# Differences of kept weights written to the exponentials' tile, at other steps, and two result rows leaving one group later

## The chip, the cores and the metric

One core of a Trainium2 chip runs the whole program. The metric is the device time of one execution in microseconds, the median of the runs shown. TensorE (PE) multiplies matrices, VectorE (DVE) and ScalarE (ACT) work element by element, GpSimd (POOL) and SyncE (SP) here only issue transfers.

## What is computed

```python
def _attn_ref(q, k, v, phi) -> np.ndarray:
...
    k_m = np.einsum('bhsm,bhsd->bhmd', a, k)
    v_m = np.einsum('bhsm,bhsd->bhmd', a, v)
...
    scores = scale * np.matmul(q, k_m.transpose(0, 1, 3, 2))
...
    return np.matmul(attn, v_m).astype(np.float32)
...
def _moe_ref(x, w_gate, w_val, w_out) -> np.ndarray:
    gate = 1.0 / (1.0 + np.exp(-(x @ w_gate)))
    val = x @ w_val
    return (gate * val @ w_out).astype(np.float32)
```

`a` is the softmax of `phi` over 32 memory slots, `attn` that of the scores. There are 8 batches of 8 heads, 576 positions, 64 wide; the attention's output is turned into 4608 tokens of 512 and goes through the gated layer of width 1536. The weights come in as 64-bit words and are turned into 32-bit floats on the chip.

## The kernel before, in words

The hidden width of 1536 is cut into 12 slices of 128. A **unit** is one batch and one slice: a gate (`gate_half`, two halves of columns), sigmoid on ACT, product on DVE (`product`, L711), rounding to a high part on ACT (`g_hi`, L721) and the rest on DVE (`g_lo`, by `rest`, L184), and later the product with the output weights into four accumulators (`out_half`). Batches 0 to 2 go through the slices in three turns of four (units 0 to 35 of `steps`); what has been summed after a turn leaves as a row (`leave`, from L766 on) to a buffer in memory and comes back as `row<-part` to be added on DVE (L771). Batches 3 to 7 then take all slices in one turn, in groups of another arithmetic (`Group`), with sums and differences of operands.

Those late batches need the gate weights once more, with the lower head of each pair as a difference of two halves. So in six of the units 0 to 35, listed in `KEEP_W`, two slices of weights are **kept**: SP issues two copies from the weights' tile (`wgv<-wg`, 512 KB and 256 KB), DVE makes two differences of 64 x 512 (L1247), and SP issues them as two transfers of 128 KB (`wgv<-row` before).

What sets the order: the first 12 units and the late batches are written out by hand. Between them, a scheduler places each engine's instructions by its own estimate of when they are ready. Each engine runs its list strictly in order, so an instruction that waits holds everything behind it. `move` (L173 to L180) issues nearly all loads and stores of this stretch on SP's queue, in program order.

Tiles come from pools with a fixed number of buffers; a new tile waits until every reader of the old one in its buffer is done. `row` has four, shared by rows that leave, rows that return, and (before) the differences. `e`, which holds the exponentials of a softmax, has one. The gates use four PSUM banks, `pu_t`: a unit's first half takes one, its second half two, so the second half of a unit takes a bank that the previous unit's first product has read. `acc0` to `acc3` are the four accumulators, one bank each, free when their row has been added (L771).

In the late loop (from L1409 on), `leave_late` adds and stores what is in `leaving`, twice per group: in the middle (L1458) and near the end (L1508).

Of the kernel before, what the change touches and what calls it, by code (L numbers as in the profile page):

```python
# [9 lines left out]
F32 = mybir.dt.float32  # L10
# [7 lines left out]
P = 128  # L18
B, H, S, D, M = 8, 8, 576, 64, 32
DM, DFF = 512, 1536  # L20
NG = 2
NKT = 4
# [18 lines left out]
QUAD = 3  # L41
# [62 lines left out]
def attn_moe_kernel(  # L104
# [15 lines left out]
    mb = ctx.enter_context(tc.tile_pool(name="moe", bufs=1))  # L120
# [19 lines left out]
    def att(shape, name, bufs=1):  # L140
        return sb.tile(shape, F32, name=name, bufs=bufs)
# [32 lines left out]
    def move(dst, src, queue="batch"):  # L174


        with ExitStack() as behind:
            if queue in last_move:
                behind.enter_context(tc.issue_after(last_move[queue].ins))
            last_move[queue] = queues[queue].dma_start(dst, src)  # L180
# [141 lines left out]
    def convert(f, k):  # L322
        to_f32(whole_of(f, k), f, k)
        if k == 2:
            wo_hi(f)
            wo_lo(f)
# [34 lines left out]
    def load_q(b, cuts=(0, 1)):  # L361
        if (b, "q") not in loaded:
            loaded[b, "q"] = att([P, NKT * S], "q")
        for c in cuts:
            for u, n in PIECES[c]:
                o = u * NKT * 2 * P
                move(loaded[b, "q"][:, o : o + NKT * n], qT[b][:, o : o + NKT * n])
# [235 lines left out]
    def again(b):  # L603
        new_at(b)
        for d, a in zip(kept[b], at[b]):
            move(a.rearrange("p r n -> p (r n)").bitcast(F32), d)
# [131 lines left out]
    def gate_all(b, f, c):  # L738
        for do in (gate_half, sigmoid, product, g_hi, g_left, g_lo):
            do(b, f, c)  # L740
# [52 lines left out]
    def row_of(b, t):  # L793

        st = mb.tile([P, DM], F32, name="row", bufs=4)
        if (b, t) in part:
            move(st, part[b, t])
        return st
# [6 lines left out]
    def out_left(pair, f0, nf):  # L805

        if pair:
            hi, lo = [mb.tile([P, TURN, P], F32R, name=f"left_{p}", tag="row", bufs=4) for p in ("hi", "lo")]
        else:
            hi, lo = [t.rearrange("p r f x -> p (r f x)").rearrange("p (f x) -> p f x", x=P) for t in u_tiles()]  # L810
        for k in range(0, nf, TURN):
            raw = left.pop((pair, (f0 + k) // TURN))
            nc.scalar.copy(hi[:, k : k + TURN], raw)
            if pair:
                yield
            rest(lo[:, k : k + TURN], raw, hi[:, k : k + TURN])
        yield
        ends_it = f0 + nf == NFT
        n = DM // 2 if ends_it and pair == B // 2 - 1 else DM
        if f0 == 0:  # L820
            left_sum[pair] = mb.tile([P, DM], F32, name="wo_raw")
        for x in range(0, DM, n):
            xs = slice(x, x + n)
            st, o = left_sum[pair][:, xs], (late_bank("c") if x else bank())[:, :n]
            for k in range(nf):
                w_hi, w_lo = [w[:, xs] for w in wo_of(f0 + k)]
                matmul(o, hi[:, k], w_hi, start=(k == 0), stop=False)
                matmul(o, hi[:, k], w_lo, start=False, stop=False)
                matmul(o, lo[:, k], w_hi, start=False, stop=(k == nf - 1))
            if "banks" in pools and n == DM:  # L830
                yield
            if f0 == 0:
                nc.vector.tensor_copy(st, o)
                continue
            nc.vector.tensor_tensor(st, o, st, op=ALU.add)
            if not ends_it:
                continue
            for j in range(2):
                b = 2 * pair + j
                to = out[b * S + SF * P : (b + 1) * S, xs]  # L840
                move(to, st[j * TAIL : (j + 1) * TAIL, :], ("batch", "act")[j] if pair == B // 2 - 1 else "batch" if pair else "stream")
        yield


    def run(*parts):
        for p in parts:
            for _ in p:
                pass
# [7 lines left out]
    @contextmanager  # L856
    def queued():

        traced = nc.cur_bb.bb.instructions
        at = traced[-1]  # L860
        with ExitStack() as behind:
            for ins in tail_of.values():
                behind.enter_context(tc.issue_after(ins))
            yield
        start = next(k for k in reversed(range(len(traced))) if traced[k] is at) + 1
        for ins in traced[start:]:
            if ins.engine in ORDERED:
                tail_of[ins.engine] = ins

    def step(do, *args, **kw):  # L870
        with queued():
            return do(*args, **kw)
# [162 lines left out]
            yield  # L1035

    MAIN = begin[QUAD, 0]
    KEEP_W = {17: 0, 18: 1, 19: 2, 20: 3, 25: 5, 28: 4}
    sides = {
        begin[0, TURN]: [(6, remember(QUAD, True))],  # L1040
        begin[1, NFT - TURN]: [(3, pause(3)), (3, score(QUAD, QUAD + 1))],
# [39 lines left out]
    def load_pair(n):  # L1081

        if n >= NPAIRS:
            return
        in_ring[n] = lp[0].tile([P, 2, NKT, 256], F32, name="ring")
        move(in_ring[n].rearrange("p f k n -> p (f k n)"), kept_w[n % NP])
# [142 lines left out]
    for i, (b, f, at_start, at_end) in enumerate(steps[:MAIN]):  # L1229
        if i < LISTED:  # L1230
            continue
        if i in sides:
            run(beside)
            beside, pieces = chain(*(g for _, g in sides[i])), sum(n for n, _ in sides[i])
            length = next(n for n in range(i + 1, len(steps) + 1) if n == len(steps) or steps[n][2]) - i
            slots = 2 * length - 1 - sum(i <= n < i + length for n in quad_at)
        if i in returns:
            again(returns[i])
        if i in KEEP_W:
            k = KEEP_W[i]  # L1240
            w, kept_k = wg[:, 2 * k : 2 * k + 2], kept_w[k].rearrange("p (f k n) -> p f k n", f=2, k=NKT)
            move(kept_k[D:], w[D:])
            move(kept_k[:D, :, :, :P], w[:D, :, :, :P])
            for j in range(2):
                t = mb.tile([P, DM], F32, name="row", bufs=4)[:D]
                t = t.rearrange("p (k n) -> p k n", k=NKT)
                nc.vector.tensor_tensor(t, w[:D, j, :, :P], w[:D, j, :, P:], op=ALU.subtract)  # L1247
                move(kept_k[:D, j, :, P:], t)
        if i == begin[1, NFT - TURN] - 1:
            load_q(QUAD)  # L1250
        if i == MAIN - 2:
            for t in range(SF):
                rows[b, t] = row_of(b, t)
        if i == MAIN - TURN:
            weights.close()
            lp[0] = weights.enter_context(tc.tile_pool(name="late2", bufs=1, side="right", reuse_waits="tile"))
            load_pair(0)
        extra = out_left(*lefts[i]) if i in lefts else iter(())
        gate_all(b, f, 0)
        due = list(CONVERT.get(i, ()))  # L1260
        while due and i not in quad_at:
            with behind():
                convert(*due.pop(0))
        next(extra, None)
        if i in u_at:
            if steps[i + 1][0] != b:
                run(beside)
            make_u(*u_at[i])
            part_u(*u_at[i])
        while len(pend) >= LAG:  # L1270
            out_half(*pend.pop(0))
        pend.append((b, f, 0, at_start, at_end))
        go_on()
        gate_all(b, f, 1)
        while due and due[0][1] != 2:
            with behind():
                convert(*due.pop(0))
        if i == MAIN - 3:
            with behind():
                first_hi(QUAD, 0)  # L1280
                first_lo(QUAD, 0)
                sums_at(QUAD, 1, 2, 3, 4)
        while len(pend) >= LAG and i < MAIN - 1:
            out_half(*pend.pop(0))
        if i in quad_at:
            quad(i)
            while due:
                with behind():
                    convert(*due.pop(0))
        if i == MAIN - 2:  # L1290
            pair_u(0, [bank(), bank()])
            for name in "rl":
                u_out(0, name)
            u_sums(0, 0, 1, 2)
            for name in "lrs":
                part_hi(0, name)
                part_lo(0, name)
        pend.append((b, f, 1, at_start, at_end))
        next(extra, None)
        if i not in quad_at:  # L1300
            go_on()
        del U[b, f]
# [109 lines left out]
    for b, f in [(b, f) for b in range(QUAD, B) for f in range(NFT)]:  # L1412
# [7 lines left out]
        n = (b - QUAD) * NP + f // 2  # L1420
# [84 lines left out]
        to_lo_done = h and b == QUAD and len(leaving) > 0  # L1505
        if to_lo_done:
            step(h.to_lo)
        step(leave_late)  # L1508
        if late_left:
            step(next, extra, None)  # L1510
        last = b == B - 1 and f == NFT - 1
# [97 lines left out]
```

## Time and profile before

| what | us |
|---|---|
| median of 3 runs (717.38 to 717.57) | 717.55 |
| the profiled execution | 718.11 |
| its span in the trace | 716.3 |
| PE busy in the span | 705.1 |
| DVE busy | 554.7 |
| ACT busy | 445.6 |
| all 16 transfer engines, mean | 172 GB/s |

The span is what the trace covers; some 1.8 us of the profiled execution's time lie around it. PE is busy 98% of the span at the full granted clock in every slice, so time can only be gained or lost where PE stands idle, or by giving it other work.

### The profile page before, as it was taken

The page shows a single profiled execution, that of the slowest core. Times are in us where ns is not written, and L with a number is a line of the kernel's source. Part 1 is how long each engine was busy: PE and PEld are TensorE (multiplying, and loading weights), DVE is VectorE, ACT ScalarE, POOL GpSimd, SP SyncE. Part 2 cuts the span into 40 slices and gives each one's busy share as a digit, 9 for nine tenths or more (in the row PEclk, how much of TensorE's full clock was granted, in tenths as well). Part 3 has the DMA queues.
Part 4 walks back from the last instruction along what each step waited for, and adds up shares of the span by engine and source line. Part 5 has one row for each costly group of instructions (what it writes and reads, how often), then busy time and mean ns, then how long its engine had stood idle before and what let it go on. Part 6 is the DMA issues. An engine that isn't in the chain of part 4 may idle for free.

```text
span 716.3 us, 14525 instructions
## 1 busy us (share of the span) xinstructions
PE 705.1 (98%) x5645; PEld 581.4 (81%) x5645; DVE 554.7 (77%) x1108; ACT 445.6 (62%) x1037; POOL 27.6 (4%) x55
## 2 busy tenths in 40 slices
PE   8999999999999999999999999999999999999997
PEld 7655898888988888878878888888888888788786
DVE  5898998778787676587888868787797778987663
ACT  4655776543354354466877567765777657686553
POOL 0000100111101110100000000000000000000000
PEclk9999999999999999999999999999999999999999
DMA  8966559878956835733166112752223422151102
GB/s 347 405 259 210 213 193 378 289 267 272 319 182 196 275 117 184 262 104 112 60 231 236 60 60 89 254 184 67 93 93 116 154 92 75 60 176 60 60 1 73
DMA packets 36084, 123.22 MB, mean 172 GB/s; under 512 B 3952, under 2 KB 11376, under 8 KB 28848
## 3 DMA queue, kind: packets, MB, share of 16 engines
q1 hardware_dynamic: 31296, 106.71, 42.2%
q0 software_dynamic: 4560, 15.47, 6.2%
q8 instruction: 44, 0.72, 0.4%
q14 instruction: 24, 0.20, 0.1%
q10 hardware_dynamic: 160, 0.13, 0.1%
HBM read 96.73 MB, written 25.56 MB: 171 GB/s over the span
## 4 chain that ended last, share of the span: by engine, by line
PE 86%; DMA 6%; DVE 4%; ACT 2%; SPq 1%; issue 1%; POOL 0%; DVEq 0%
PE acc L194 36%; PE pu_t L194 17%; PE c L194 11%; PE a L194 8%; PE b L194 7%; PE d L194 7%; DMA kvm<-in_kvm_dram 2%; DMA words<-in_wo_dram 1%; DMA row<-part 1%; DMA out_dram<-row 1%; SPq L180 1%; DMA part<-row 1%; DVE row L771 1%; DVE u_lo L184 1%; DVE row L1247 0%
## 5 line engine op out<-in xcount | busy, mean ns | idle before, releaser
L194 PE MATMUL acc<-wo_hi,g_hi 128*128 128x512 f32 x372 | 151.4, 407 | 0.0
L194 PE MATMUL acc<-wo_hi,g_lo 128*128 128x512 f32 x372 | 147.1, 395 | 0.0
L194 PE MATMUL acc<-wo_lo,g_hi 128*128 128x512 f32 x372 | 146.7, 394 | 0.0
L194 PE MATMUL pu_t<-at,u_hi 128*128 128x320 f32 (+1 forms) x560 | 116.7, 305 | 1.1 <-DVE e L512 1.1
L194 PEld LDWEIGHTS pu_t<-at,u_hi 128*128 128x128 f32 x560 | 92.1, 188 | 9.8 <-issue 2.1
L194 PEld LDWEIGHTS acc<-wo_hi,g_hi 128*128 128x128 f32 x372 | 69.8, 188 | 29.4 <-issue 9.7
L194 PEld LDWEIGHTS acc<-wo_hi,g_lo 128*128 128x128 f32 x372 | 69.9, 188 | 17.4 <-DVE g_lo L184 0.3
L194 PE MATMUL pu_t<-at,u_lo 128*128 128x256 f32 (+1 forms) x264 | 77.6, 294 | 0.0
L194 PEld LDWEIGHTS acc<-wo_lo,g_hi 128*128 128x128 f32 x372 | 70.1, 188 | 5.4
L1197 ACT COPY c_p<-c 128x288 f32<-128x288 f32 x60 | 23.9, 398 | 63.1 <-PE c L194 62.4
L169 ACT ACTIVATE sg<-pu_t 128x256 f32<-128x256 f32 (+1 forms) x70 | 28.5, 410 | 50.8 <-PE pu_t L194 46.5
L1201 DVE TENSOR_TENSOR z<-a,c_s 128x288 f32<-128x288 f32 x60 | 27.1, 452 | 32.9 <-PE a L194 32.8
L194 PEld LDWEIGHTS pu_t<-at,u_lo 128*128 128x128 f32 x264 | 49.6, 188 | 0.0
L721 ACT CAST g_hi<-sg 128x256 fp32r<-128x256 f32 x66 | 26.5, 405 | 36.5 <-DVE sg L711 34.6
L711 DVE TENSOR_TENSOR sg<-pu_t,sg 128x320 f32<-128x320 f32 (+1 forms) x69 | 31.1, 454 | 23.3 <-ACT sg L169 13.8
L169 ACT ACTIVATE z<-z 128x288 f32<-128x288 f32 x120 | 47.9, 441 | 1.5 <-DVE z L1201 0.8
L1201 DVE TENSOR_TENSOR z<-c,c_x 128x288 f32<-128x288 f32 x60 | 27.3, 455 | 27.3 <-PE c L194 24.5
L1213 ACT CAST g_hi<-z 128x512 fp32r<-128x512 f32 x60 | 37.4, 623 | 17.0 <-DVE z L1208 16.8
L184 DVE TENSOR_TENSOR g_lo<-z,g_hi 128x512 fp32r<-128x512 f32 x60 | 41.0, 684 | 2.5 <-ACT g_hi L1213 2.5
L194 PE MATMUL c<-ring,vT 64*32 64x512 f32 x232 | 31.4, 601 | 0.0
L194 PE MATMUL a<-ring,vT 64*32 64x512 f32 x232 | 31.4, 601 | 0.0
L1208 DVE TENSOR_TENSOR z<-z 128x288 f32<-128x288 f32 x60 | 27.0, 450 | 5.4 <-ACT z L169 0.8
(243 smaller groups left out, 1636.8 us busy)
## 6 DMA issues: line engine op xcount, KB each, us to landing
ring<-wgv SPq DMA_DIRECT2D x30, 1024.0 KB, 4.9
kvm<-in_kvm_dram SPq DMA_DIRECT2D x14, 1024.0 KB, 8.8
at<-at SPq DMA_DIRECT2D x18, 576.0 KB, 8.1
q<-in_qT_dram SPq DMA_DIRECT2D x16, 512.0 KB, 4.9
part<-row POOLq DMA_DIRECT2D x24, 256.0 KB, 5.0
row<-part SPq DMA_DIRECT2D x24, 256.0 KB, 3.8
words<-in_wo_dram SPq DMA_DIRECT2D x8, 512.0 KB, 9.6
words<-in_wgv_dram SPq DMA_DIRECT2D x4, 1024.0 KB, 5.1
```

Of the source, the lines that this page charges most:

```text
L169: last_act[0] = nc.scalar.activation(*args, **kw)
L180: last_move[queue] = queues[queue].dma_start(dst, src)
L184: return nc.vector.tensor_tensor(lo, x, hi.bitcast(F32), op=ALU.subtract)
L194: last_pe[0] = do(*args, **kw)
L711: last_prod[0] = nc.vector.tensor_tensor(prod, ps[1][:, :n], sg[:, :n], op=ALU.mult)
L721: nc.scalar.copy(hi, prod[:, : 2 * P])
L771: nc.vector.tensor_tensor(st, o, st, op=ALU.add)
L1197: copy(getattr(self, name), self.c if name == "p5" else self.d)
L1201: nc.vector.tensor_tensor(self.z[:, i], x, y, op=ALU.add)
L1208: nc.vector.tensor_tensor(self.z[:, 2 + i], x, self.z[:, i], op=ALU.mult)
L1213: nc.scalar.copy(self.g[0], self.z[:, 2:4, : 2 * P])
```

## The change

`KEEP_W` gives the unit at which a pair of slices is kept. Pair 4 moves from unit 28 to unit 22; the other five stay. The two differences of a pair now lie side by side in one tile of the name `e`, with one buffer, in place of two of the four `row` buffers. And in group 1 of batch 3, the late call of `leave_late` is left out, so the two rows that wait there leave at the call in the middle of group 2.

```diff
-    KEEP_W = {17: 0, 18: 1, 19: 2, 20: 3, 25: 5, 28: 4}
+    KEEP_W = {17: 0, 18: 1, 19: 2, 20: 3, 22: 4, 25: 5}
...
             move(kept_k[D:], w[D:])
             move(kept_k[:D, :, :, :P], w[:D, :, :, :P])
+            diff = att([P, 2 * S], "e")[:D, : 2 * DM].rearrange("p (f k n) -> p f k n", f=2, k=NKT)
             for j in range(2):
-                t = mb.tile([P, DM], F32, name="row", bufs=4)[:D]
-                t = t.rearrange("p (k n) -> p k n", k=NKT)
+                t = diff[:, j]
                 nc.vector.tensor_tensor(t, w[:D, j, :, :P], w[:D, j, :, P:], op=ALU.subtract)
                 move(kept_k[:D, j, :, P:], t)
...
-        step(leave_late)
+        if (b, f) != (QUAD, 1):
+            step(leave_late)
```

The instructions of PE keep their order, row for row. DVE's list moves at three places. The first is on DVE around the begin of unit 16: `u_lo` x4 are the rests of the operands of units 16 to 19, the next `sg` of 256 is unit 16's first product, the four rows from `acc_1682` on are the sums of batch 0 that leave. Before:

```order
L184 TENSOR_TENSOR u_lo<-pu_t,u_hi 128x512 x4
L711 TENSOR_TENSOR sg<-pu_t,sg 128x256
L273 TENSOR_SCALAR wg<-wg 128x512
L276 TENSOR_SCALAR wg<-wg 128x512
L184 TENSOR_TENSOR g_lo<-sg,g_hi 128x256
L711 TENSOR_TENSOR sg<-pu_t,sg 128x320
L280 SCALAR_TENSOR_TENSOR wg<-words_90,wg 128x512
L771 TENSOR_TENSOR row<-acc_1682,row 128x512
L771 TENSOR_TENSOR row<-acc_1686,row 128x512
```

And now, from the same `u_lo` on:

```order
L184 TENSOR_TENSOR u_lo<-pu_t,u_hi 128x512 x4
L1247 TENSOR_TENSOR e<-wg 64x512 x2
L711 TENSOR_TENSOR sg<-pu_t,sg 128x256
L273 TENSOR_SCALAR wg<-wg 128x512
L711 TENSOR_TENSOR sg<-pu_t,sg 128x320
L276 TENSOR_SCALAR wg<-wg 128x512
L771 TENSOR_TENSOR row<-acc_1682,row 128x512
L184 TENSOR_TENSOR g_lo<-sg,g_hi 128x256
L771 TENSOR_TENSOR row<-acc_1686,row 128x512
L280 SCALAR_TENSOR_TENSOR wg<-words_90,wg 128x512
L184 TENSOR_TENSOR g_lo<-sg,g_hi 128x256
L1247 TENSOR_TENSOR e<-wg 64x512 x2
```

The second and the third pair of differences (pairs 1 and 2) now stand here; before, the first pair came 21 rows after this `u_lo`. Pair 0 now stands before it, 10 rows up. After the third come a product, the row from `acc_1760`, two weight instructions, and the row from `acc_1764`.

The second place is on DVE in unit 20, again behind the four `u_lo` of a new turn. Before:

```order
L711 TENSOR_TENSOR sg<-pu_t,sg 128x320
L280 SCALAR_TENSOR_TENSOR wg<-words_90,wg 128x512
L771 TENSOR_TENSOR row<-acc_2054,row 128x512
L771 TENSOR_TENSOR row<-acc_2058,row 128x512
L184 TENSOR_TENSOR g_lo<-sg,g_hi 128x256
```

And now:

```order
L711 TENSOR_TENSOR sg<-pu_t,sg 128x320
L1247 TENSOR_TENSOR e<-wg 64x512 x2
L280 SCALAR_TENSOR_TENSOR wg<-words_90,wg 128x512
L771 TENSOR_TENSOR row<-acc_2053,row 128x512
L771 TENSOR_TENSOR row<-acc_2057,row 128x512
```

The differences of pair 4 stand ahead of two rows that free accumulators. The first differences in this neighbourhood stood behind all four such rows before.

The third place is on DVE in groups 1 and 2 of batch 3. Before:

```order
L184 TENSOR_TENSOR g_lo<-z,g_hi 128x512
L771 TENSOR_TENSOR row<-acc_3397,row 128x512
L771 TENSOR_TENSOR row<-acc_3401,row 128x512
L1201 TENSOR_TENSOR z<-b,c_p_3699 128x288
L184 TENSOR_TENSOR u_lo<-s_raw,u_hi 128x768
```

And now:

```order
L184 TENSOR_TENSOR g_lo<-z,g_hi 128x512
L1201 TENSOR_TENSOR z<-b,c_p_3693 128x288
L184 TENSOR_TENSOR u_lo<-s_raw,u_hi 128x768
L512 STREAM_TRANSPOSE e<-b 128x224
L512 STREAM_TRANSPOSE e<-d 128x224
L1208 TENSOR_TENSOR z<-z 128x288
L771 TENSOR_TENSOR row<-acc_3391,row 128x512
L771 TENSOR_TENSOR row<-acc_3395,row 128x512
```

The two rows stand five instructions later, behind the transposes of a softmax. The differences that stood on DVE right ahead of the four transposes `e<-pu_t` (unit 28's, pair 4) are gone from there.

## Rows read from the trace of the kernel before

**Rows 1.** The profile's page, busy time, share of the span, instructions.
```profile
PE 705.1 (98%) x5645; PEld 581.4 (81%) x5645; DVE 554.7 (77%) x1108; ACT 445.6 (62%) x1037; POOL 27.6 (4%) x55
```

**Rows 2.** Waits of PE: who waited for whom, us in total, times, longest.
```profile
PE b L194 <- DVE z L1201: 1.3, 1, 1.3
...
PE pu_t L194 <- DVE e L512: 1.1, 1, 1.1
```

**Rows 3.** Timeline, 238 to 252 us: start, us, instruction, idle before and its releaser.
```profile
242.03 1.31 DVE L1247 TENSOR_TENSOR row<-wg 64x512 f32<-64x512 f32 x2 [2.37 <-DMA out_dram<-row]
...
243.61 1.56 DVE L512 STREAM_TRANSPOSE e<-pu_t 128x288 f32<-128x288 f32 x4
...
244.13 0.50 PE L194 MATMUL pu_t<-at,u_hi 128*128 128x256 f32 x2 [1.08 <-DVE e L512]
```

**Rows 4.** Timeline, 299 to 316 us, the same columns.
```profile
305.94 1.28 DVE L771 TENSOR_TENSOR row<-acc,row 128x512 f32<-128x512 f32 x2
...
307.64 0.37 PE L194 MATMUL b<-q,kT 64*32 64x224 f32 x1 [1.26 <-DVE z L1201]
...
310.28 0.46 DVE L1201 TENSOR_TENSOR z<-a,c_s 128x288 f32<-128x288 f32 x1 [0.86 <-PE a L194]
```

**Rows 5.** Line 1247: engine, count, ns min/median/max, first and last start.
```profile
L1247 DVE TENSOR_TENSOR row<-wg x12: 672/682/684, 164.6 to 242.7; 64x512 f32<-64x512 f32 x12
```

**Rows 6.** Timeline of DVE, 140 to 160 us.
```profile
150.21 2.48 DVE L184 TENSOR_TENSOR u_lo<-pu_t,u_hi 128x512 fp32r<-128x512 f32 x4
153.82 0.43 DVE L711 TENSOR_TENSOR sg<-pu_t,sg 128x256 f32<-128x256 f32 x1 [1.13 <-ACT sg L169]
...
156.52 1.28 DVE L771 TENSOR_TENSOR row<-acc,row 128x512 f32<-128x512 f32 x2
...
158.98 0.69 DVE L771 TENSOR_TENSOR row<-acc,row 128x512 f32<-128x512 f32 x1
```

**Rows 7.** Timeline of PE, 150 to 168 us.
```profile
159.09 0.46 PE L194 MATMUL pu_t<-at,u_hi 128*128 128x320 f32 x2
...
160.86 0.39 PE L194 MATMUL acc<-wo_hi,g_hi 128*128 128x512 f32 x1
...
163.67 0.39 PE L194 MATMUL acc<-wo_hi,g_hi 128*128 128x512 f32 x1
```

**Rows 8.** Timeline of SP's queue, 146 to 182 us: start and length of issues.
```profile
147.81 1.21 SPq L180 DMA_DIRECT2D wgv<-wg  x2
...
177.87 2.25 SPq L180 DMA_DIRECT2D row<-part  x4
...
181.13 1.93 SPq L180 DMA_DIRECT2D wgv<-wg  x2
```

**Rows 9.** Transfers issued 147.3 to 149.1 us: KB each, us from issue to landing.
```profile
wgv<-wg SPq DMA_DIRECT2D x1, 512.0 KB, 8.0
wgv<-wg SPq DMA_DIRECT2D x1, 256.0 KB, 9.1
```

**Rows 10.** The same, issued 165.2 to 166.2 us.
```profile
wgv<-row SPq DMA_DIRECT2D x2, 128.0 KB, 4.6
```

**Rows 11.** The same, issued 221 to 223 us.
```profile
wgv<-row SPq DMA_DIRECT2D x2, 128.0 KB, 2.4
```

**Rows 12.** The same, issued 180 to 182 us.
```profile
wgv<-wg SPq DMA_DIRECT2D x1, 512.0 KB, 9.6
...
wgv<-wg SPq DMA_DIRECT2D x1, 256.0 KB, 14.3
```

**Rows 13.** Timeline of DVE, 181 to 191 us.
```profile
182.43 1.28 DVE L771 TENSOR_TENSOR row<-acc,row 128x512 f32<-128x512 f32 x2
...
190.62 0.68 DVE L1247 TENSOR_TENSOR row<-wg 64x512 f32<-64x512 f32 x1 [3.78 <-DMA part<-row]
```

**Rows 14.** Timeline of PE, 185 to 192 us.
```profile
186.78 0.39 PE L194 MATMUL acc<-wo_hi,g_hi 128*128 128x512 f32 x1
```

**Rows 15.** Busy time by stretch; last columns granted clock, transfer share, GB/s.
```profile
140.00:150.00 10.00, 10.00 (x83) 7.78 (x81) 6.09 (x13) 4.86 (x13) 0.55 (x1) 1.00 1.00 384
```

## Prediction

> **What bounds the kernel.** I read the busy times first: PE works in 98% of the span [rows 1], so this program is a row of matrix products with few holes, and a change elsewhere counts only if it closes a hole or opens one. Then the waits of PE. Behind the start-up, two are left that are over 1 us [rows 2], and both name DVE, which is in order. The timeline says what DVE did there. At 242 us it stood 2.37 us before two differences (L1247), because a `row` buffer was still being stored to the output; the four transposes that free the gates' banks stood behind, and PE lost 1.08 us [rows 3]. At 306 us two leaving rows took 1.28 us ahead of the sum `z` that PE's next product waited for; PE lost 1.26 us [rows 4]. The change aims at just these two. What it puts in their place has to be read in the stretch from 150 to 200 us, where PE waits for nothing now: there I read how late each thing may come.
>
> **What it gives.** At 242 us no difference stands any more, and the transposes can run as soon as the scores are there. I count the hole of 1.08 in full, as 1.1. At 306 us `z` now follows the product's rest at once, some 1.2 earlier (the two rows' 1.28 less their overlap), out of a hole of 1.26. Sum of the gain: **2.3 us** (2.1 to 2.4). The two rows themselves, 1.28 us, move to where DVE stood idle for 0.86 us before its next sum [rows 4]; the 0.4 left over delays a sum that PE is not waiting for. I cost it at nothing; without that cover it is 0.4.
>
> **What it adds.** No instruction is new: twelve differences of 0.68 us [rows 5] before and now. New is their wait. With one buffer, a pair of differences can't begin before both transfers of the pair before it have landed. And the list of DVE now has pairs 1 and 2 early, ahead of products and of rows that free accumulators; whatever the pair waits, these wait too.
>
> *The first wait (pair 1, behind `u_lo` x4).* DVE gets there at 150.21 + 2.48 = 152.7 [rows 6]. When do the transfers of pair 0 land? SP's queue issues them right behind the two copies of that pair, at about 149.1 and 149.7; the copies went out at 147.81 and 148.4 [rows 8] and landed 8.0 and 9.1 us later, at 155.8 and 157.5 [rows 9]. The transfer engines are full there, at 384 GB/s and a share of 1.00 [rows 15], and the landings follow the order of issue. So the two pieces come after 157.5. The 256 KB copy, in pieces of the same size, came 1.7 after the one ahead of it; the two together are another 256 KB, which gives 159.2 as the late end. I take X = 158.5. DVE stands still for 5.8 us.
>
> What is queued behind, step by step, with the lengths of these rows less their small overlaps. The pair takes 1.2, the product 0.42: the bank is free at 160.1. PE asks for it at 159.09 [rows 7], now 4.8 us after the product's end at 154.25 [rows 6]: late by 1.0. The first leaving row ends at X + 3.3 = 161.8; PE wants its accumulator at 160.86 + 1.0 [rows 7]: just in time; the second row, 0.95 behind where PE moves on by 0.7, costs 0.25. Then pair 2, at X + 5.1 = 163.6, waits for pair 1's transfers: issued at 160.4 at the latest, 2.4 us if nothing else runs [rows 11], 4.6 with traffic [rows 10], so 162.9 to 165.0, say 164.0. The third row ends at 166.2 where PE wants 163.67 + 1.25 [rows 7]: 1.3. The fourth, with two weight instructions ahead, comes 1.6 later where PE moves on by 0.7: 0.9. Sum: **3.5 us**. With X = 157.5 and pair 1's transfers at their shortest it is 2.2, with X = 159.2 and the longest 4.8.
>
> *The second wait (pair 4, unit 20).* It needs pair 3's transfers. SP can't issue those before the reloads of rows and operands of that turn; I leave that group at 181 us [rows 8], which puts the two pieces at 182.0 and 182.6. Before, the copies ahead of them landed 9.6 and 14.3 us after issue, at 190.7 and 195.9 [rows 12]. The 14.3 came with four row stores and two weight loads on POOL's queue in the same stretch; now those stores come behind the differences in question, so they are absent. I take the landing Y = 191. The early end is 187.5: the group's four reloads, two operands, two copies and two pieces are 3.2 MB, from 177.87 on [rows 8] at 384 GB/s [rows 15], and 1.3 us to begin. The late end is 195.9 + 1.7 = 197.6. Here two leaving rows stand behind the pair: the first ends at Y + 2.4. It ended at 183.1 before [rows 13], and PE wanted its accumulator at 186.78 [rows 14], so at 190.3 with the 3.5 from above. Loss: Y + 2.4 - 190.3 = Y - 187.9 = **3.1 us** (0 to 9.7). The same stretch shows why DVE's wait of 3.78 us before was free [rows 13]: it stood behind all four rows, and the pair ahead of them is the difference. Later pairs (3 and 5) have their transfers landed, or stand where PE is already later by more than they wait: nothing. Pair 4's own copies and transfers, now six units earlier, stand on SP's queue ahead of the reloads of the next turn and hold them until the differences are done. Of those, the operands are read four units later, and the rows are wanted at that turn's end: nothing, and if that cover were gone, the second wait would show a second time.
>
> **The sum.** 3.5 + 3.1 - 2.3 = +4.3 us. The profiled execution's own 718.11 (its span of 716.3 and 1.8 around it) becomes 722.4. It stands 0.56 above the median of the runs, so against the median of 717.55 I say **721.9**. About 0.2%, 1.4 us, is what a measurement of this kernel can tell from no change.
>
> **A rule against my reading.** That pair 0's pieces land only after the copies ahead of them is read from the order of landings [rows 9]. The Trainium skill, in "DMA: Bandwidth & Descriptors" (section "Queues, rings and completion order"), says that completion is not first in, first out per issuing engine. The transfers of SP's queue in this trace do land in order, which is the case that the rule doesn't promise; by the rule a time near the first rival's would be possible.
>
> **Rivals.**
> 1. *Faster.* The pieces don't stand in line: they land 4.6 us after issue as other pieces did [rows 10], at 154.3. DVE then waits 1.6 and the product ends 1.7 later than before, against a slack of 4.8; pair 4's land at 187.2, before 187.9. The holes opened are nothing, and 717.55 - 2.3 = 715.3. The point that decides: X below 157.5 and Y below 187.9. For it speak the pieces before, with 2.4 and 4.6 us [rows 10, 11]; against it, that DVE made each of those late, so that little stood ahead of it. 0.12.
> 2. *Only the first wait shows.* With POOL's stores out of the way Y is at its early end: 3.5 - 2.3 = +1.2, 718.8. With the first wait's lower end it is no change at all. 0.14, of which I count 0.10 within 0.2%.
> 3. *The second wait is as long as it can be.* Y = 197.6: 3.5 + 9.7 - 2.3 = +10.9, 728.5. For it speaks the copy of 14.3 us [rows 12]. 0.08.
>
> That the change doesn't do what it says is excluded for its two aims: the order of DVE shows both sets of instructions gone from ahead of what PE waited for.
>
> **How the numbers follow.** My forecast, both waits in part, has 0.66. Faster by over 0.2%: rival 1, 0.12. Within 0.2%: 0.10 from rival 2. Slower: 0.66 + 0.04 + 0.08 = 0.78. The range has to hold the forecast and rival 2: from 718.0 (the first wait at 2.8, the second at nothing) to 726.0 (the first at 3.5, the second at 7.2). It leaves out rival 1 and rival 3, 0.20. The cases of one sign hold most of it, so it needs no second range.
>
> **What would show it.** In the profile after: no wait of PE for a transpose `e` near 242 us and none of 1.26 near 306; a wait of DVE L1247 for `wgv<-e` of 5 to 6 us ending near 158, one of 4 to 6 us near 190; and new waits of PE on a gate's bank and on accumulators (DVE L1247's followers: the product, the rows, and ACT's rounding behind them) between 159 and 170 and near 190 to 195. If L1247 waits under 2 us at 153, or PE shows no wait from 150 to 200 us, the argument has failed; if PE waits as said but the total is lower, the price of one of the two waits was wrong.

## The result and the profile after

| what | before | after |
|---|---|---|
| median of the runs beside each other (4 and 4), us | 717.56 | 725.63 |
| lowest and highest, us | 717.38, 717.91 | 724.70, 727.83 |
| the profiled execution, us | 718.11 | 724.70 |
| its span, us | 716.3 | 722.9 |

The ratio is 1.0116, with a 95% interval of 1.0093 to 1.014: the change makes the kernel 8 us slower. The forecast was 721.9 in a range of 718.0 to 726.0, slower with a chance of 0.78.

The page of the kernel after, busy times: DVE, ACT and POOL do the same work as in [rows 1], and PE is busy 3.2 us longer with the same 5645 products.

```profile
PE 708.3 (98%) x5645; PEld 582.8 (81%) x5645; DVE 555.0 (77%) x1108; ACT 446.0 (62%) x1037; POOL 28.1 (4%) x55
```

The waits of PE after. The two of [rows 2], on `z` and on `e`, are gone from the list. New are waits on a leaving row, which frees an accumulator, and on a product, which frees a gate's bank.

```profile
PE acc L194 <- DVE row L771: 5.6, 4, 3.7
...
PE pu_t L194 <- DVE sg L711: 0.3, 1, 0.3
```

The differences after (line 1247: count, ns min/median/max, first and last start), and what DVE stood idle for ahead of them. Their length is that of [rows 5]; two waits for the differences' own transfers make 12.2 us.

```profile
L1247 DVE TENSOR_TENSOR e<-wg x12: 677/682/698, 142.1 to 203.5; 64x512 f32<-64x512 f32 x12
...
its engine sat idle before it (us, times) until:
  DMA wgv<-e: 12.2, 2
```

DVE's timeline after, 148 to 196 us. The pair behind `u_lo` starts at 158.32 and the pair in unit 20 at 191.00, each behind 6.1 us of idle time; the products and rows that stood at 153.82 to 158.98 in [rows 6] and at 182.43 in [rows 13] follow them.

```profile
149.75 2.48 DVE L184 TENSOR_TENSOR u_lo<-pu_t,u_hi 128x512 fp32r<-128x512 f32 x4
...
158.32 1.29 DVE L1247 TENSOR_TENSOR e<-wg 64x512 f32<-64x512 f32 x2 [6.08 <-DMA wgv<-e]
...
163.39 1.29 DVE L1247 TENSOR_TENSOR e<-wg 64x512 f32<-64x512 f32 x2
...
191.00 1.29 DVE L1247 TENSOR_TENSOR e<-wg 64x512 f32<-64x512 f32 x2 [6.14 <-DMA wgv<-e]
...
192.82 1.27 DVE L771 TENSOR_TENSOR row<-acc,row 128x512 f32<-128x512 f32 x2
```

PE's timeline after. Five holes answer to these two waits, where [rows 7, 14] had none; the last, of 3.75 us, stands ahead of the first accumulator of unit 20. The rows from 195.13 on show what follows it: the products of 256 columns that take 0.40 us a pair elsewhere take 0.63.

```profile
159.99 0.57 PE L194 MATMUL pu_t<-at,u_hi 128*128 128x320 f32 x2 [0.31 <-DVE sg L711]
...
161.75 0.47 PE L194 MATMUL acc<-wo_hi,g_hi 128*128 128x512 f32 x1 [0.60 <-DVE row L771]
...
165.76 0.47 PE L194 MATMUL acc<-wo_hi,g_hi 128*128 128x512 f32 x1 [0.79 <-DVE row L771]
...
167.20 0.51 PE L194 MATMUL acc<-wo_hi,g_hi 128*128 128x512 f32 x1 [0.51 <-DVE row L771]
...
193.64 0.47 PE L194 MATMUL acc<-wo_hi,g_hi 128*128 128x512 f32 x1 [3.75 <-DVE row L771]
...
195.13 0.63 PE L194 MATMUL pu_t<-at,u_hi 128*128 128x256 f32 x2
...
198.52 0.40 PE L194 MATMUL acc<-wo_hi,g_lo 128*128 128x512 f32 x1
```

Busy time by stretch after; the last columns are granted clock, transfer share and GB/s. Between 194 and 199 us the mean granted clock is 0.66, so part of the stretch ran at the lower level, 1.2 GHz.

```profile
190.00:194.00 4.00, 0.36 (x2) 0.35 (x3) 3.00 (x5) 0.00 (x0) 0.21 (x1) 1.00 0.65 207
194.00:199.00 5.00, 5.00 (x23) 4.49 (x22) 5.00 (x13) 1.48 (x5) 3.06 (x6) 0.66 0.69 215
```

PE runs the same products in the same order in both kernels, so the start of each can be compared with its own before. Just ahead of the first wait the profiled execution after is 0.45 us early, from its start-up. Then it stands so:

| product | before, us | after, us | later by | step |
|---|---|---|---|---|
| `pu_t<-at,u_hi` ahead of the first wait | 159.09 [rows 7] | 158.64 | -0.45 | |
| last of the four accumulators there | 164.35 | 167.20 | 2.85 | first wait +3.3 |
| first accumulator of unit 20 | 186.78 [rows 14] | 193.64 | 6.86 | second wait +4.0 |
| end of the stretch of slow products | 190.04 | 198.52 | 8.48 | clock +1.6 |
| products behind the transposes | 244.13 [rows 3] | 251.35 | 7.22 | first hole closed, -1.25 |
| scores of group 2 | 307.64 [rows 4] | 313.57 | 5.93 | second hole closed, -1.3 |

In sum 3.3 + 4.0 + 1.6 - 2.55 = 6.35 us from the first wait to the last row of the table. With the 0.45 by which this execution was early that is 5.9 us; the spans differ by 6.6, and the other 0.7 lies behind 314 us, 0.2 of it where the late rows now stand (below, "The late rows alone") and 0.4 behind PE's last product. The medians lie 8.1 apart: the profiled execution after is the fastest of its four, which differ among each other by 3 us.

### The profile page after: what moved, and what is told of

Same layout as the page of the kernel before. It is cut to its first block, busy times and chain, and to the rows that moved or that the text cites. A ratio compares the mean times of both kernels' runs of the same rounds, so it can differ in the third digit from the quotient of the medians.

```text
span 722.9 us, 14531 instructions
## 1 busy us (share of the span) xinstructions
PE 708.3 (98%) x5645; PEld 582.8 (81%) x5645; DVE 555.0 (77%) x1108; ACT 446.0 (62%) x1037; POOL 28.1 (4%) x55
## 4 chain that ended last, share of the span: by engine, by line
PE 88%; DMA 5%; DVE 3%; ACT 2%; issue 1%; SPq 1%; DVEq 0%; ACTq 0%
PE acc L194 37%; PE pu_t L194 18%; PE c L194 10%; PE a L194 8%; PE b L194 7%; PE d L194 7%; DMA wgv<-e 2%; DMA kvm<-in_kvm_dram 2%; DMA words<-in_wo_dram 1%; SPq L180 1%; DVE row L771 0%; ACT L164 0%; DVE wg L280 0%; DVE e L1247 0%; DVE wg L285 0%
## 5 line engine op out<-in xcount | busy, mean ns | idle before, releaser
L184 DVE TENSOR_TENSOR g_lo<-sg,g_hi 128x256 fp32r<-128x256 f32 x66 | 27.3, 418 | 5.5 <-ACT g_hi L721 5.4
```

The costliest lines, as they stand in the source:

```text
L184: return nc.vector.tensor_tensor(lo, x, hi.bitcast(F32), op=ALU.subtract)
```

## The experiments

The theory: one buffer of `e`, and an order of DVE that puts pair 1 and pair 4 ahead of what PE wants, cost 3.3, 4.0 and 1.6 us; the two closed holes give 2.5. The rivals: that pair 4's new place costs by itself, that the late rows cost, or that one buffer costs wherever its pairs stand. Each kernel was run beside the kernel before (29 runs of it for a group of four kernels; their median is 717.49 for the late rows, the tile for pairs 0 to 2, that for pairs 3 to 5 and each pair held back, and 717.14 for the other four). The differences in us below are those of the ratio, and the difference of two medians can be up to 1 us off it. "Aligned" below means: each product of PE against the same one of the profiled execution of the kernel before, as in the table above.

### The late rows alone

The kernel before with the third edit alone:

```diff
-        step(leave_late)
+        if (b, f) != (QUAD, 1):
+            step(leave_late)
```

> The kernel before with the late leave alone left out in group 1 of batch 3; keeping of weights as before. Theory: the hole of PE of 1.26 us at 306 us closes and nothing else changes: 717.56 - 1.3 = 716.3 (716.0 to 716.6), ratio 0.998; the hole of 1.08 at 242 us stays. Rival (the two rows, a group later, hold up something else): 717.5 or more.

716.67 us, ratio 0.9984 (0.9969 to 0.9999): -1.1 us, where -1.3 was expected. Aligned, PE gains 1.14 at the products that followed the hole at 306 us. The late rows are a gain, not a cost. Their new place is not quite free: in all eight kernels that have them, the loading of weights for PE waits 0.33 or 0.34 us for a rest `g_lo` there, PE loses 0.2, and the kernel with the move alone shows neither.

```profile
314.71 0.19 PEld L194 LDWEIGHTS acc<-wo_hi,g_lo 128*128 128x128 f32 x1 [0.34 <-DVE g_lo L184]
```

One thing was wrong: the hole at 242 us was not there either. In this profiled execution the start-up ended 2.4 us later (the last section shows why), but the output store that the differences wait for let them go only 1.2 later, at 243.22 against 242.03: DVE waited 0.94 us for it instead of the 2.37 of [rows 3], and PE lost nothing.

DVE in this run, the same place as [rows 3]:

```profile
243.22 0.68 DVE L1247 TENSOR_TENSOR row<-wg 64x512 f32<-64x512 f32 x1 [0.94 <-DMA out_dram<-row]
```

### The move alone

The kernel before with pair 4 at its new unit:

```diff
-    KEEP_W = {17: 0, 18: 1, 19: 2, 20: 3, 25: 5, 28: 4}
+    KEEP_W = {17: 0, 18: 1, 19: 2, 20: 3, 22: 4, 25: 5}
```

> The kernel before with pair 4 at unit 22 alone (row buffers, and the two rows leave as before). Theory: the hole of 1.08 at 242 us closes, that of 1.26 at 306 stays, nothing opens: 1.1 us below the runs of before beside it, ratio 0.9985 (0.997 to 1.000). Rival: a new hole at the new place, and no gain.

716.78 us, ratio 0.9991 (0.9978 to 1.0005): -0.6 us, not told apart from no change, and from -1.1 neither. Aligned, the whole difference is one step of -1.24 at the products behind the transposes, and nothing opens elsewhere.

### The tile undone alone

The kernel after, the differences in row buffers again:

```diff
-            diff = att([P, 2 * S], "e")[:D, : 2 * DM].rearrange("p (f k n) -> p f k n", f=2, k=NKT)
...
-                t = diff[:, j]
+                t = mb.tile([P, DM], F32, name="row", bufs=4)[:D].rearrange("p (k n) -> p k n", k=NKT)
```

> The kernel after with the tile undone alone: all differences in row buffers as before; pair 4 stays at unit 22 and the two rows still leave a group later. Theory: the losses hang on the one buffer of e and on where DVE's order puts its pairs. With four row buffers the order up to unit 20 is that of before, so no wait stands ahead of PE's needs, and both holes are closed (1.1 to 1.25 each): 2.5 us below the runs of before beside it, ratio 0.9965 (0.995 to 0.998), clock 1.00. Rival (pair 4's copies and transfers at unit 22 cost the time): PE waits between 186 and 200 us stay, ratio 1.004 or more.

716.00 us, ratio 0.9979 (0.9965 to 0.9992): -1.5 us. This is the fastest of all versions. From 60 us on PE has no wait that the view lists. The edit takes the tile out of the change, with the order of DVE that the scheduler makes for it, and takes all of the loss with it; pair 4 at unit 22 costs nothing by itself. The gain is smaller than the 2.5 expected, though the interval just holds it; aligned, the profiled execution does gain 1.25 and 1.2 at the two places. The run of the late rows shows why the median can gain less: the first hole is not in every execution.

The waits of PE in this kernel over its whole span, the last three of seven; all seven belong to the start-up:

```profile
PE pu_t L194 <- ACT scrap L164: 0.5, 1, 0.5
PE acc L194 <- DVE at L577: 0.3, 1, 0.3
PE pu_t L194 <- DVE wg L285: 0.2, 1, 0.2
```

### The tile for pairs 0 to 2 alone

The kernel after, with row buffers for pairs 3 to 5:

```diff
-            diff = att([P, 2 * S], "e")[:D, : 2 * DM].rearrange("p (f k n) -> p f k n", f=2, k=NKT)
+            if k < 3:
+                diff = att([P, 2 * S], "e")[:D, : 2 * DM].rearrange("p (f k n) -> p f k n", f=2, k=NKT)
...
-                t = diff[:, j]
+                t = diff[:, j] if k < 3 else mb.tile([P, DM], F32, name="row", bufs=4)[:D].rearrange("p (k n) -> p k n", k=NKT)
```

> The kernel after, with pairs 0 to 2 in the tile e as in the change and pairs 3 to 5 in row buffers as before. DVE's order up to unit 19 is that of the change; in unit 20 all four leaving rows stand ahead of the next difference. Theory: the first wait alone is left: 717.56 + 3.3 - 2.5 = 718.4 (717.8 to 719.4); DVE waits about 6 us for the transfers of pair 0 up to 158, PE loses 0.9, 0.2, 1.0 and 0.8 between 159 and 170, nothing of note from 186 to 200, and the granted clock stays at 1.00, since no hole of PE is longer than 1.1 us. Rival (the second loss and the lower clock come from pair 4's move to unit 22, whatever tile it uses): 724 or more, with a clock below 1.00 near 195.

719.15 us, ratio 1.0024 (1.0012 to 1.0036): +1.7 us against the runs beside it, where +0.8 was expected (3.3 - 2.5). Aligned, the first wait costs 3.8 us, the two holes give 1.25 and 1.2, and nothing stands between. So the first wait is isolated. The second loss and the lower clock behind it are not there. In 12 runs the mean clock is 0.999 or 1.000 in ten; two with 0.995 and 0.996 took 721.51 and 719.75 us, and no trace shows where their clock fell. PE's holes are those of the kernel after, at the same four places:

```profile
160.67 0.57 PE L194 MATMUL pu_t<-at,u_hi 128*128 128x320 f32 x2 [0.80 <-DVE sg L711]
...
162.43 0.47 PE L194 MATMUL acc<-wo_hi,g_hi 128*128 128x512 f32 x1 [0.60 <-DVE row L771]
```

And by stretch, the clock at full where the kernel after had 0.66:

```profile
170.00:200.00 30.00, 30.00 (x203) 25.84 (x202) 25.03 (x54) 12.80 (x33) 5.44 (x10) 1.00 0.86 291
```

### The tile for pairs 3 to 5 alone

The same edit with `k > 2`.

> The kernel after, with pairs 0 to 2 in row buffers as before and pairs 3 to 5 in the tile e. The order now puts pair 3's differences early (its tile is free) and pair 4's behind all four leaving rows of unit 20. Theory: neither wait stands ahead of anything that PE wants, both old holes stay closed: 717.56 - 2.5 = 715.1 (714.8 to 716.0), clock 1.00. Rival (pair 4's transfers at unit 22, or the tile e itself, cost the time): no faster than 717.5.

724.54 us, ratio 1.0097 (1.0076 to 1.0117): the forecast for this run was wrong by 9 us. No wait stands ahead of the rows, as the order said; but pair 4, behind all four rows, waits 14.15 us for pair 3's transfers, and behind it stands the rest `g_lo` that PE wants at 192.5. One hole of 9.0 us takes the place of five.

DVE's wait in this run:

```profile
199.78 1.29 DVE L1248 TENSOR_TENSOR e<-wg 64x512 f32<-64x512 f32 x2 [14.15 <-DMA wgv<-e]
```

PE's hole:

```profile
201.45 0.80 PE L194 MATMUL acc<-wo_hi,g_lo 128*128 128x512 f32 x1 [8.98 <-DVE g_lo L184]
```

Transfers issued between 180 and 183 us (KB, us from issue to landing): the first of pair 3's two pieces took 15.9 us.

```profile
part<-row POOLq DMA_DIRECT2D x1, 256.0 KB, 7.5
wgv<-e SPq DMA_DIRECT2D x1, 128.0 KB, 15.9
```

In the kernel after the same piece took 7.8 us from an issue at 182.7:

```profile
wgv<-e SPq DMA_DIRECT2D x1, 128.0 KB, 7.8
```

What differs between the two is, above all, what POOL's queue had in flight. Here four row stores and two loads of 512 KB were issued there from 182.52 to 187.7; in the kernel after DVE stood ahead of the rows, and POOL's next store went out at 193.79. SP's own queue differs less: when the piece went out, two reloads of 256 KB were still in flight here, and in the kernel after none; at 384 GB/s [rows 15] they make 1.4 us of the 8. This is the third rival of the prediction, with its Y of 197.6 surpassed, in a kernel where the rows do not wait. The two runs agree with it; no edit changed POOL's stores alone. The Trainium skill, "DMA: Bandwidth & Descriptors" (section "Queues, rings and completion order"), says that each transfer engine takes turns between the queues that have work for it, which fits: a second busy queue takes part of every turn. No run here shows the turns themselves.

### The move undone alone

The kernel after with pair 4 back at its old unit:

```diff
-    KEEP_W = {17: 0, 18: 1, 19: 2, 20: 3, 22: 4, 25: 5}
+    KEEP_W = {17: 0, 18: 1, 19: 2, 20: 3, 25: 5, 28: 4}
```

> The kernel after with the move undone alone: pair 4 back at unit 28, the tile e and the late leave stay. The first wait is as in the change (3.3 us of PE). In unit 20 the next difference is now pair 5's first; it stands ahead of the last of the four leaving rows and waits for pair 3's transfers just as pair 4 did. Theory: with three rows already on their way out, those transfers land later, as in the run with pairs 3 to 5 in e (13 us or more after issue, near 198 to 201), the last row is 6 to 9 us late, and the granted clock falls behind that hole (another 1.6): 717.5 + 3.3 - 1.3 + 7.5 + 1.6 = 728.6 (722 to 731). Rival (the move of pair 4 makes the second loss): with the move undone only the first wait is left, 718.3 to 719.8, clock 1.00.

728.43 us, ratio 1.0149 (1.012 to 1.0179); the profiled execution took 731.64, with 2.5 us more in its start-up than that of before. The total is as forecast and the rival falls, but the way is another one. Aligned, the first wait costs 3.4; the last row of unit 20 costs only 1.8, not 6 to 9; two operands of the output weights, behind another wait of DVE for the transfers (4.31 us, at 217), are late by 2.4; and the dearest place is a new one. Pair 4's pieces leave the tile `e` at unit 28, and the softmax's transposes write into that very tile: they wait 5.86 us for the pieces, PE loses 2.5 beyond the hole that the kernel before has there, and the clock another 1.5.

DVE at that place, which answers to [rows 3]:

```profile
256.35 1.58 DVE L512 STREAM_TRANSPOSE e<-pu_t 128x288 f32<-128x288 f32 x4 [5.86 <-DMA wgv<-e]
```

PE there, and its clock behind it:

```profile
256.89 0.80 PE L194 MATMUL pu_t<-at,u_hi 128*128 128x256 f32 x2 [3.56 <-DVE e L512]
```

```profile
257.00:262.00 5.00, 5.00 (x26) 4.95 (x27) 4.04 (x7) 1.31 (x3) 0.00 (x0) 0.67 0.21 65
```

So with the tile `e`, pair 4 at unit 28 costs no less than at unit 22 (the intervals of the two ratios overlap), and the move belongs to the tile.

### Each pair held back

The kernel after; `behind` keeps an instruction from being placed ahead of the last product, rounding, operand and weight instruction that were written before it:

```diff
+                with behind():
-                nc.vector.tensor_tensor(t, w[:D, j, :, :P], w[:D, j, :, P:], op=ALU.subtract)
+                    nc.vector.tensor_tensor(t, w[:D, j, :, :P], w[:D, j, :, P:], op=ALU.subtract)
```

> The kernel after, with each pair of differences kept from being placed ahead of the unit in which it is written (it may not come before the last product, rounding, operand and weight instruction issued by then). One tile e as in the change. Theory: it is the place in DVE's order that costs, not the one buffer by itself. No pair stands behind the u_lo of unit 16 and none ahead of the four leaving rows of unit 20, so the losses of 3.3, 4.0 and 1.6 us (clock) go, the gain of 2.5 stays: 715.1; with pairs 0 to 3 now closer to each other a pair can still wait for the transfers of the one before (2.4 to 9 us from issue), so up to 2 us on top: 715.1 to 717.1. Rival (one buffer costs wherever the pairs stand): DVE's waits of some 6 us only move, and the time stays at 720 or above.

718.44 us, ratio 1.0016 (1.0005 to 1.0028): +1.1 us, above the range expected, and well below the 720 of the rival. The waits ahead of the rows and the second loss are gone, and aligned nothing opens before 174 us. But three pairs now stand within 16 us, and pair 2 waits 4.82 us for pair 1's transfers at 174.56, with two products behind it. PE loses 3.1 between 174 and 181 us, and gains 1.25 and 1.2 later. The place in the order explains most of the loss, one buffer with pairs close to each other the rest.

```profile
174.56 1.29 DVE L1248 TENSOR_TENSOR e<-wg 64x512 f32<-64x512 f32 x2 [4.82 <-DMA wgv<-e]
```

### Pairs 1 and 2 alone held back

The same edit, with `with behind() if k in (1, 2) else ExitStack():`.

> The kernel after with pairs 1 and 2 alone kept from being placed ahead of their unit. The order then has pair 1 behind all four rows of unit 16, pair 3 ahead of the u_lo of unit 20, and pair 4 between the first and the second of the four rows there. Theory: no first wait. At the second place PE comes 3.3 us earlier than in the kernel after, and pair 3's transfers, issued some 1.5 us earlier with one row store on its way, land at 189.5 to 191; the second row ends at 191.4 to 193 where PE wants it at 188: 3.4 to 5 us of PE, with the clock's 0 to 1.6 behind it, less the 2.5 gained: 718.4 to 721.6, one hole of PE of 3 to 5 us. Rival (the two waits add up, each worth what it cost in the kernel after): 4.0 + 1.6 - 2.5, 720.6, with the transfers landing no earlier than 191. Second rival (without the first wait the transfers land early enough): under 1 us of hole, 715 to 716.

720.01 us, ratio 1.0025 (1.0009 to 1.004). The twelve runs fall into two halves: six with a mean clock of 0.999 or 1.000 took 717.6 to 719.6 us, six with 0.996 to 0.998 took 720.4 to 720.8, the profiled execution (720.67) among these. The total fits the first line of the expectation and the place does not. Pair 4 does not wait at all: it starts at 187.36 right behind a row. The hole of 2.97 us is at 180.46, where pair 3 waits for pair 2's transfers ahead of `u_lo`.

DVE, 173 to 188 us:

```profile
177.92 1.29 DVE L1248 TENSOR_TENSOR e<-wg 64x512 f32<-64x512 f32 x2 [2.97 <-DMA wgv<-e]
179.73 2.47 DVE L184 TENSOR_TENSOR u_lo<-pu_t,u_hi 128x512 fp32r<-128x512 f32 x4
...
187.36 1.27 DVE L1248 TENSOR_TENSOR e<-wg 64x512 f32<-64x512 f32 x2
```

Why pair 4 is in time, by SP's timeline of this run:

```profile
171.86 3.62 SPq L180 DMA_DIRECT2D row<-part  x4
...
178.71 3.72 SPq L180 DMA_DIRECT2D wgv<-e  x2
```

And by that of the kernel after:

```profile
171.85 8.45 SPq L180 DMA_DIRECT2D row<-part  x4
...
182.68 2.67 SPq L180 DMA_DIRECT2D wgv<-e  x2
```

The four reloads go to the four `row` buffers that the turn's rows are stored from, so they wait for the stores. In the kernel after, the first wait delays those rows, and the weight instructions between them; POOL, which issues a load of weights ahead of each two stores, issued the stores at 167.28 and 172.81 (here at 159.48 and 164.02). So the reloads take 4.8 us longer to issue, and pair 3's pieces behind them start 4 us later. SP's waits for these stores between 165 and 185 us, in the kernel after; here there are none in that stretch:

```profile
SPq L180 <- DMA part<-row: 13.4, 4, 6.5
```

By these timelines the second wait is in part made by the first; no run delays the stores alone.

The clock behind this hole, by stretch:

```profile
180.00:184.00 4.00, 3.54 (x17) 3.54 (x18) 2.62 (x5) 0.94 (x2) 0.00 (x0) 0.62 1.01 342
```

## Why the prediction was right

**What bounds the kernel.** Right. Everything that moved the time is a hole of PE or the lower clock behind one, and each of the profile's signs that the prediction named is there: no hole near 242 or 306, two waits of L1247 (it said 5 to 6 us near 158 and 4 to 6 near 190; 6.08 and 6.14 are measured, ending at 158.32 and 191.00, both a little over), and holes on a gate's bank and on accumulators in the two stretches named.

**The gain**, 2.3 us: 2.55 in the profiled execution. Counting the first hole in full was right for this execution and too much for the median: the kernel without the tile gains 1.5 (0.6 to 2.5).

**The first wait**, 3.5 us: 3.3, and 3.4 and 3.8 in two other kernels with the same order. X, the landing of pair 0's pieces, was set at 158.5; the pair starts at 158.32. The reading that the pieces land behind the copies issued ahead of them holds: they took 8.6 us. With it the first rival falls (X of 154.3), and the prediction's "rule against my reading" does not show: in both traces every transfer of SP's queue lands in order of issue. The single terms are less exact than their sum: aligned, the bank costs 0.5 and the four rows 0.9, 0.3, 0.9 and 0.8, where 1.0, 0, 0.25, 1.3 and 0.9 were forecast. The bank was read as asked for at 159.09, but PE runs that product unhindered at 158.64 and asks for the bank 0.9 us later; what this charged too much came back at the first row. Pair 2 did not wait at all, since pair 1's pieces took 2.5 us.

**The second wait**, 3.1 us: 4.0. Y was set at 191, and the pair starts at 191.00. That this moment came out is in part luck. The prediction took the reloads and the copies to leave SP's queue when they left it before, from 177.87 on, behind the transfers of the differences. In the kernel after those are gone from there, and the reloads start 6 us earlier, at 171.85; what held them until 180.3 was the stores that the first wait had delayed, a link that the prediction did not see. So the pieces went out at 182.68, where 182.0 was set; with pairs 1 and 2 held back they went out at 178.71. The early end of Y rests, besides, on 1.3 us "to begin" that no row shows. What was off in the price is the moment at which PE wants its accumulator, taken as 186.78 + 3.5 = 190.3. PE was there at 193.64 - 3.75 = 189.89: the first wait cost it less, and this execution had begun 0.45 earlier, while the transfers had not come earlier with it. The row ended a little later than Y + 2.4, too, and between the two rows of the table PE falls back 0.25 more than the hole itself (6.86 - 2.85 = 4.0 against 3.75).

What stood ahead of the reloads on SP's queue before:

```profile
174.29 3.48 SPq L180 DMA_DIRECT2D wgv<-row  x2
```

**What was left out**: the granted clock. The prediction priced a hole at its length. Behind the hole of 3.75 us PE ran part of the next 5 us at 1.2 GHz, which cost another 1.6 us; this term, with the 0.9 missing from the second wait, makes the difference between the sum forecast, +4.3, and the 6.35 of the two profiled executions (the gain and the first wait, off by 0.2 each, take back 0.4). The rest up to the medians' 8.1 is 0.2 at the two ends of the span and 1.5 of spread between executions, which one trace does not show.

**The range.** The time lies 0.4 us below its upper end. That end stood for a second wait of 7.2 us, and the second wait was 4.0: the clock, which the prediction left out, and the spread filled the rest, so that the time fell inside is in part luck. Rival 2 (718.8) is the kernel with the first wait alone, 719.15, and rival 3's late landing is that of the run with pairs 3 to 5 in `e`: both mechanisms exist, in other orders than this change's. Of what the prediction priced at nothing, pair 4's copies at unit 22 cost nothing (the kernel with row buffers has no wait of PE from 60 us on that the view lists), and the two rows in their later place cost 0.2.

## What to carry to other kernels

A buffer that is emptied by a transfer is free when the transfer lands, and behind busy queues that was 7 to 16 us here, not the 2.4 that the same transfer took in a quiet stretch; before sharing a tile, ask what stands in order behind its next writer. Where a scheduler places such a writer early by its own estimate, read the resulting order of the engine: the loss hung on whether a pair stood ahead of or behind a row that PE wanted. And a hole of PE is not to be priced at its length alone: those of about 3 us and more cost 1.5 to 1.7 us on top here, by the lower clock that came with them.

## What the runs showed of the hardware

Every hole of PE of about 3 us or more in these traces was followed or accompanied by a stretch at the lower granted clock: 2.97 (mean clock 0.62 over the 4 us from 180), 3.56 (0.67 over 257 to 262), 3.75 (0.66 over 194 to 199) and 8.98. From the first product behind the hole to the end of the slow stretch, PE fell back 1.6, 1.5, 1.6 and, for the longest, 1.7 us. Of twelve runs of the kernel with the hole of 2.97 us, with pairs 1 and 2 held back, six show a mean clock of 0.999 or more, and their middle (718.3) is 2.3 us below that of the other six (720.6); only one of the twelve is traced, so what their holes were is not known. Holes of 1.53 us and less (in the runs with the move undone and with pairs 0 to 2 in `e`) left it at 1.00. In the longest the clock was down while PE still stood:

```profile
196.00:201.00 5.00, 0.00 (x0) 0.00 (x0) 1.22 (x3) 0.00 (x0) 0.00 (x0) 0.50 0.27 93
201.00:206.00 5.00, 4.55 (x19) 4.08 (x20) 5.00 (x14) 2.16 (x6) 0.00 (x0) 0.59 0.76 217
```

Two start-ups show the same, with the late rows alone and with the move undone: PE waits 2.94 and 2.78 us for a load of `kvm`, the mean clock over the 4 us from 18 is 0.57 and 0.58, and the start-up ends 2.4 to 2.5 us later than that of the kernel before, whose clock is 1.00 there. No edit touches this place, so it differs between executions. With the late rows alone:

```profile
16.80 1.08 PE L194 MATMUL pu_t<-kvm,row 128*32 128x128 f32 x32 [2.94 <-DMA kvm<-in_kvm_dram]
```

```profile
18.00:22.00 4.00, 4.00 (x40) 2.75 (x40) 3.11 (x4) 0.00 (x0) 0.00 (x0) 0.57 1.04 412
```

Some of the spread of one kernel may come from there. Of the 58 runs of the kernel before, the seven with a mean clock of 0.998 or less took 719.27 to 720.98 us, and only two of the others took over 718.7. So a low mean clock of a run doesn't tell by itself which hole lowered it, in the halves above either.

Also not expected: a hole of over 1 us that the trace of one execution shows, the one at 242 us, was absent in another execution of the same products whose start-up ended 2.4 us later. The store that DVE waited for there came only 1.2 us later; why it does not move with PE is not tried.
